# Decode attention and MLP on one core: K tiles two heads ahead of V tiles, one turn moved ahead of the last values, and five matmuls into a spare tile

## The chip, the cores and the metric

The kernel runs on one core of one Trainium2 chip. The metric is the device time of one execution in microseconds (us); lower is better. The profile's span, from the first to the last instruction, is about 1.8 us shorter than that time, because it leaves out what comes before and after. The profiled execution is one of the timed ones, so its own time is known.

Engines in the profile: PE is the matmul engine, PEld its weight loads (they overlap PE), DVE the vector engine, ACT the scalar engine, SP the engine whose queue issues the loads. In the timelines below, the instructions of one engine start in the order of the program.

## The reference, cut to what matters

A decode step, four rows of 576 values: attention over a window of 2048 cached positions, 16 KV heads of 128 with two query heads each, plus an MLP block on the same normalised input.

```python
def _A_ref(x, k_cache, v_cache, wq, wo):                       # attention
    q = (x @ wq).reshape(B, Sq, 32, 128).transpose(0, 2, 1, 3)
    k = jnp.repeat(k_cache[:, :, Sk - W:, :], 2, axis=1)         # W = 2048
    v = jnp.repeat(v_cache[:, :, Sk - W:, :], 2, axis=1)
    p = _softmax(jnp.einsum("bhqd,bhkd->bhqk", q, k) * 128 ** -0.5, axis=-1)
    o = jnp.einsum("bhqk,bhkd->bhqd", p, v)
    return o.transpose(0, 2, 1, 3).reshape(B, Sq, 4096) @ wo
# ... the MLP: x1 = x + shifted part (with one token: zeros); x1 + gelu(layernorm(x1) @ w3) @ w4
return x + _A_ref(xn, ...) + _B_ref(xn, ...)                   # xn = layernorm(x)
```

K and V of the window are 32 tiles of 2 MB (2048 KB each in the profile); with the weights the kernel loads 87.17 MB.

## The kernel before

Loads go through one queue in a fixed order. K and V tiles share six buffers. The order is made here:

```python
order = [("K", 0), ("K", 1), ("K", 2)]
for h in range(Hkv):                       # Hkv = 16
    order.append(("V", h))
    if h + 3 < Hkv:
        order.append(("K", h + 3))         # so: ... K14 V12 K15 V13 V14 V15, then w4
W4_PIECES = [0, 18, 24, 30, 34, 35, 36]    # w4 comes in six loads, the last two of 144 KB
```

A step `t` of the main loop computes scores of head `t`, the softmax of head `t-1` and the product with V of head `t-2`, in four slices. The order of the emissions is the order on each engine:

```python
for t in range(Hkv):
    hm, hv, hf, hp = t - 1, t - 2, t - 3, t - 4
    for s in range(NSL):                   # NSL = 4
        ...
        k_transpose(*divmod(t * NSL + s + 1, NSL))   # DVE: turns the NEXT slice of K ("kt")
        if s == 0:
            if hm >= 0: sm_max(hm)         # DVE: maximum of the scores ("mx", "dm")
            ...
            k_mask(t)
        elif s == 1 and hm >= 0:
            sm_maxT(hm)                    # PE: "mg", needs dm
        ...
        if hv >= 0: pv(hv, s)              # PE: P times V ("O"), needs the V tile
        k_scores(t, s)                     # PE: "S", needs kt
        ...
```

After the last step comes the tail. `hl` is head 15:

```python
    sm_max(hl); sm_rec(hl - 1); o_scale(hl - 2)
    pv(hl - 1, 0); sm_maxT(hl); sm_neg(hl); pv(hl - 1, 1); sm_sub(hl); sm_exp(hl)
    o_turn(hl - 2); pv(hl - 1, 2); pv(hl - 1, 3); o_sum(hl - 2)
    sm_turn(hl); sm_den(hl); sm_rec(hl)    # DVE: PT, which pv(hl) needs
    o_scale(hl - 1)                        # ACT: O_sb of head 14
    for s in range(NSL):
        pv(hl, s)                          # PE: the values of head 15
    o_scale(hl)                            # ACT: O_sb of head 15
    o_turn(hl - 1); o_sum(hl - 1)          # PE: turn ("oT") of head 14; DVE: "on"
    o_turn(hl); o_sum(hl)
    o_spread(hl)                           # PE: "R"
    o_pick(hl)                             # DVE: "mk", "op"
    mlp_out(*pieces[0])                    # PE: 36 matmuls with w4's first piece
    o_proj(hl)                             # PE: 16 matmuls with wo, needs op
    mlp_out(*pieces[1]); mlp_out(*pieces[2]); mlp_out(*pieces[3])
    # ... ACT copies one of two accumulators; pieces 4 and 5 (4 matmuls); DVE adds; store
```

Of the kernel before, what the change touches and what calls it, by code (L numbers as in the profile page):

```python
# [12 lines left out]
F32 = mybir.dt.float32  # L13
# [9 lines left out]
def kernel(  # L23
# [14 lines left out]
    nc = tc.nc  # L38
    P = 128
    B, Sq, D = A_x.shape  # L40
    _, Hkv, Sk, Dh = A_k_cache.shape
# [18 lines left out]
    NW = SC * QD  # L60
# [24 lines left out]
    ps_s = ctx.enter_context(tc.tile_pool(name="ps_s", bufs=2, space=PSUM))  # L85
# [5 lines left out]
    w_tiles = {}  # L91
# [64 lines left out]
    def cleared(shape, name):  # L156
        t = const.tile(shape, BF16, name=name)
        flat = t[:] if len(shape) == 2 else t[:].rearrange("p a b -> p (a b)")
        flat = flat.bitcast(F32)
        nc.scalar.activation(out=flat, in_=zero[:].bitcast(F32).to_broadcast(list(flat.shape)), func=ACT.Copy)  # L160
        return t
# [5 lines left out]
    OR = NI * B  # L167
    OW = OR + NI
    ROWS = slice(NI - 1, NI - 1 + OR, NI)
    gT = cleared([P, NF, OW], "gT")  # L170
# [8 lines left out]
    def acc_matmuls(terms):  # L179
        for i in range(NI):  # L180
            for n, (lhsT, rhs) in enumerate(terms):
                to, q, start = (second[0], QD, second[1]) if second and n % 2 else (acc, 0, False)
                nc.tensor.matmul(out=to[q:q + OR, :], lhsT=lhsT[:, NI - 1 - i:NI - 1 - i + OR],  # L183
                                 rhs=rhs[:, i * CW:(i + 1) * CW], start=start, stop=False, skip_group_check=True)
                if start:
                    second[1] = False
# [119 lines left out]
    for ie in range(4):  # L306
        ib, e = divmod(ie, 2)
        nc.tensor.matmul(out=qs_ps[:, :, ie], lhsT=sel[:, ib, e].rearrange("p k i -> p (k i)"),
                         rhs=q_bf.rearrange("p r g u b -> p (r g u b)"), start=True, stop=True)
# [69 lines left out]
    def sm_rec(h):  # L379
        rd = small.tile([P, 1], F32, tag="rd", bufs=4)  # L380
        nc.vector.reciprocal(out=rd[:], in_=st.pop(("dn", h))[:])
        st["rd", h] = rd

    def pv(h, s):
        if s == 0:
            O_ps[h] = ps_o.tile([P, NSL, Dh], F32, tag="O", name="O")
        vn = kv_tiles["V", h][:].rearrange("p (s c) d -> p s c d", s=NSL)
        for g in range(NQD):
            c = s * NQD + g
            nc.tensor.matmul(out=O_ps[h][g * QD:(g + 1) * QD], lhsT=PT[h][:, c, :], rhs=vn[:, :, c, :],  # L390
                             start=(s == 0), stop=False, skip_group_check=True)
        if s == NSL - 1:
            PT.pop(h)

    def o_scale(h):
        O_sb[h] = bigp.tile([P, NSL, Dh], F32, tag="big", name="O_sb")
        nc.scalar.activation(out=O_sb[h][:], in_=O_ps.pop(h)[:], func=ACT.Copy, scale=st.pop(("rd", h))[:, 0:1])  # L397

    def o_turn(h):
        oT = ps_m.tile([P, NSL, P], F32, tag="m", name="oT")  # L400
        o = O_sb.pop(h)
        for s in range(NSL):
            nc.tensor.transpose(out=oT[:, s, :], in_=o[:, s, :], identity=ident_w[:, s * NJ:s * NJ + P])  # L403
        st["oT", h] = oT

    def o_sum(h):
        oT = st.pop(("oT", h))
        v = oT[:].rearrange("p s (g x) -> p (s g) x", g=NQD)[:, :, 0:NJ].rearrange("p g (b r) -> p b r g", r=rep)
        k = h % WOQ
        if k == 0:  # L410
            st["on"] = small.tile([P, WOH, B], BF16, tag="on", name="on")
        with nc.allow_low_precision("summed in float32"):
            nc.vector.reduce_sum(out=st["on"][:, k * rep:(k + 1) * rep, :].rearrange("p r b -> p b r"),  # L413
                                 in_=v, axis=AX.X)
# [22 lines left out]
    def o_proj(h):  # L437
        if h % WOQ < WOQ - 1:
            return
        for i in range(0, WOR, 2):  # L440
            acc_matmuls([(op[:, i + u, :], wo_tiles[h // WOQ][:, i + u, :]) for u in range(2)])
# [43 lines left out]
    def mlp_out(lo, hi):  # L485
        w4 = w_tiles["w4"]
        for i in range(lo, hi, 2):
            acc_matmuls([(gT[:, u, :], w4[:, u, :]) for u in range(i, min(i + 2, hi))])


    order = [("K", 0), ("K", 1), ("K", 2)]
    for h in range(Hkv):
        order.append(("V", h))
        if h + 3 < Hkv:
            order.append(("K", h + 3))
    W3_AFTER = ("V", 2)
    pos = {"n": 0, "free": NKV}

# [17 lines left out]
# [3 lines that stand above are left out]
            if s == NSL - 1 and hm >= 0:  # L519
                sm_turn(hm)  # L520
            n = t * NSL + s + 1
# [47 lines left out]
    hl = Hkv - 1  # L569
# [14 lines left out]
    sm_den(hl)  # L584
    sm_rec(hl)
    o_scale(hl - 1)
    for s in range(NSL):
        pv(hl, s)
    o_scale(hl)
    o_turn(hl - 1)  # L590
    o_sum(hl - 1)
    pieces = list(zip(W4_PIECES, W4_PIECES[1:]))
    acc_odd = ps_acc.tile([P, CW], F32, tag="g", name="acc_odd")
    second += [acc_odd, True]
# [3 lines left out]
    o_pick(hl)  # L598
    mlp_out(*pieces[0])
    o_proj(hl)  # L600
    mlp_out(*pieces[1])
    mlp_out(*pieces[2])
    mlp_out(*pieces[3])
    second.clear()
    odd = const.tile([OR, CW], F32)
# [39 lines left out]
```

## Time and profile before

| | before |
|---|---|
| time, median of 3 runs at first (6 with the later ones) | 211.63 us (211.54 to 212.5) |
| span of the profiled execution (211.62 us) | 209.8 us |
| PE busy, DVE busy | 71%, 57% |
| loaded, rate over the span | 87.17 MB, 415 GB/s |
| landed: K15, V13 | 179.80, 184.61 us |
| landed: w4's six pieces | 200.48, 202.55, 204.61, 206.00, 206.41, 206.78 us |

The landing times are the last of the sixteen semaphore increments of a load, as the trace records them. The first fence has lines of the profile page of the kernel before: the busy share in 40 equal slices of 5.2 us, in tenths (for PEclk, the granted PE clock in tenths), and the chain of work that ended last, as shares of the span by engine and by line.

```profile
PE   0287496869694009659899599977994926989884
PEclk9999589696969556958999979997999985969999
DMA  7999999999999999999999999999999999999991
DMA 72%; PE 18%; DVE 6%; ACT 1%; issue 1%; SPq 0%; DVEq 0%
DMA vn<-in_A_v_cache_dram 35%; DMA w_sb<-in_B_w_dram 31%; PE S L338 7%; DMA wq_sb<-in_A_wq_dram 6%; DVE kt L225 3%; PE acc L183 2%; PE g_ps L456 2%; PE q_ps L285 2%; PE O L390 2%; PE oT L403 1%; DVE qz L317 1%; PE gT_ps L468 1%; DVE mx L344 1%; PE S L360 1%; ACT q_sb L296 1%
```

The DMA engines are full in every slice but the first and the last, and the chain is mostly waiting for loads. The Trainium skill ("DMA: Bandwidth & Descriptors", "Where 436 GB/s comes from") gives 435 GB/s as the ceiling of the ports into on-chip memory; steady slices of this trace show about 428. So the kernel is bound by its transfers until near the end. What a change of order can touch is the tail.

The next fence is the timeline of PE in the tail of the kernel before. Columns: start, duration, engine, line, operation, output<-inputs, form, count, and in brackets how long PE was idle just before and what ended that.

```profile
184.65 0.57 PE L390 MATMUL O<-vn,PT 128*32 128x512 bf16 x4 [1.55 <-DMA vn<-in_A_v_cache_dram]
185.15 1.89 PE L338 MATMUL S<-kt,qz 128*128 128x512 bf16 x4
186.97 0.18 PE L351 MATMUL mg<-dm,sel_jb 128*8 128x16 bf16 x1
194.41 0.40 PE L390 MATMUL O<-vn,PT 128*32 128x512 bf16 x4
197.92 1.05 PE L390 MATMUL O<-vn,PT 128*32 128x512 bf16 x16
198.90 0.66 PE L403 MATMUL oT<-ident_w,O_sb 128*128 128x128 f32 x4
199.81 0.66 PE L403 MATMUL oT<-ident_w,O_sb 128*128 128x128 f32 x4 [0.26 <-ACT O_sb L397]
200.85 0.35 PE L422 MATMUL R<-on,sel_wo 128*128 128x32 bf16 x8 [0.38 <-DVE on L413]
```

The last step begins when V13 lands at 184.6 (first row) and ends at 194.41, where the tail's first values (head 14) start. The second row: four score matmuls took 1.89 us, while elsewhere they take 1.07. PE was at half clock there. The end of the chain of waits of the same kernel (start, duration, what):

```profile
174.94 31.06 DMA w_sb<-in_B_w_dram
206.00 0.04 issue
206.04 0.28 PE acc L183
...
206.74 0.41 ACT odd L606
```

The last thing that PE waits for is the load of w4's fourth piece. PE was ready for it only about 0.2 us earlier.

### The profile page before, as it was taken

The page shows a single profiled execution, that of the slowest core. Times are in us where ns is not written, and L with a number is a line of the kernel's source. Part 1 is how long each engine was busy: PE and PEld are TensorE (multiplying, and loading weights), DVE is VectorE, ACT ScalarE, POOL GpSimd, SP SyncE. Part 2 cuts the span into 40 slices and gives each one's busy share as a digit, 9 for nine tenths or more (in the row PEclk, how much of TensorE's full clock was granted, in tenths as well). Part 3 has the DMA queues.
Part 4 walks back from the last instruction along what each step waited for, and adds up shares of the span by engine and source line. Part 5 has one row for each costly group of instructions (what it writes and reads, how often), then busy time and mean ns, then how long its engine had stood idle before and what let it go on. Part 6 is the DMA issues. An engine that isn't in the chain of part 4 may idle for free.

```text
span 209.8 us, 2403 instructions
## 1 busy us (share of the span) xinstructions
PE 149.9 (71%) x955; PEld 62.8 (30%) x955; DVE 120.4 (57%) x217; ACT 33.9 (16%) x64; POOL 2.8 (1%) x15
## 2 busy tenths in 40 slices
PE   0287496869694009659899599977994926989884
PEld 0133132223231003214364143332532401425362
DVE  3741899584831082816706869995299471771421
ACT  7602201020211000202102121120111110202300
POOL 4010000000000000000000000000000000000000
PEclk9999589696969556958999979997999985969999
DMA  7999999999999999999999999999999999999991
GB/s 301 400 412 437 428 428 428 436 422 428 469 408 420 433 428 427 438 431 428 431 437 428 422 425 446 425 425 436 422 436 428 421 435 440 425 425 448 418 402 72
DMA packets 6659, 87.32 MB, mean 416 GB/s; under 512 B 748, under 2 KB 1016, under 8 KB 1656
## 3 DMA queue, kind: packets, MB, share of 16 engines
q1 hardware_dynamic: 6640, 87.17, 97.5%
q8 instruction: 7, 0.11, 0.2%
q14 instruction: 4, 0.03, 0.0%
q10 hardware_dynamic: 8, 0.00, 0.0%
HBM read 87.17 MB, written 0.00 MB: 415 GB/s over the span
## 4 chain that ended last, share of the span: by engine, by line
DMA 72%; PE 18%; DVE 6%; ACT 1%; issue 1%; SPq 0%; DVEq 0%
DMA vn<-in_A_v_cache_dram 35%; DMA w_sb<-in_B_w_dram 31%; PE S L338 7%; DMA wq_sb<-in_A_wq_dram 6%; DVE kt L225 3%; PE acc L183 2%; PE g_ps L456 2%; PE q_ps L285 2%; PE O L390 2%; PE oT L403 1%; DVE qz L317 1%; PE gT_ps L468 1%; DVE mx L344 1%; PE S L360 1%; ACT q_sb L296 1%
## 5 line engine op out<-in xcount | busy, mean ns | idle before, releaser
L225 DVE STREAM_TRANSPOSE kt<-kn 128x1024 int32<-128x1024 int32 x64 | 76.4, 1217 | 10.9 <-DMA kn<-in_A_k_cache_dram 10.6
L338 PE MATMUL S<-kt,qz 128*128 128x512 bf16 x256 | 79.7, 441 | 3.1 <-DVE kt L225 3.1
L390 PE MATMUL O<-vn,PT 128*32 128x512 bf16 x256 | 27.4, 426 | 38.9 <-DMA vn<-in_A_v_cache_dram 37.1
L338 PEld LDWEIGHTS <-qz 128*128 128x128 bf16 x256 | 21.7, 104 | 41.5 <-issue 25.8
L366 ACT ACTIVATE E<-S 128x512 bf16<-128x512 f32 x16 | 9.5, 597 | 122.6 <-PE S L360 122.6
L390 PEld LDWEIGHTS <-PT 128*32 128x32 bf16 x256 | 7.2, 94 | 47.3 <-issue 30.2
L372 DVE STREAM_TRANSPOSE PT<-E 128x512 bf16<-128x512 bf16 x16 | 11.4, 710 | 14.9 <-ACT E L366 14.9
L356 DVE TENSOR_REDUCE nm<-mg 8x1 bf16<-8x16 f32 x16 | 2.4, 152 | 20.7 <-PE mg L351 20.7
L397 ACT ACTIVATE O_sb<-O,rd 128x512 f32<-128x512 f32 x16 | 11.0, 686 | 15.6 <-issue 11.0
L413 DVE TENSOR_REDUCE on<-oT 128x8 bf16<-128x128 f32 x16 | 4.5, 280 | 12.7 <-PE oT L403 12.7
L403 PE MATMUL oT<-ident_w,O_sb 128*128 128x128 f32 x64 | 11.1, 302 | 0.3 <-ACT O_sb L397 0.3
L344 DVE TENSOR_REDUCE mx<-S 128x1 f32<-128x512 f32 x16 | 10.5, 657 | 1.3 <-PE S L338 1.3
L403 PEld LDWEIGHTS oT<-ident_w,O_sb 128*128 128x128 f32 x64 | 9.2, 161 | 5.3 <-issue 2.9
L183 PE MATMUL acc<-wo_sb,op 128*8 128x288 bf16 x56 | 7.5, 286 | 0.0
L376 PEld LDWEIGHTS dn<-rs,same_j 128*128 128x128 f32 x32 | 5.8, 188 | 2.9 <-ACT E L366 0.7
L360 PE MATMUL S<-nm,j_row 8*128 8x512 bf16 x16 | 6.5, 409 | 0.0
L329 PE MATMUL S<-negbig,ohT 4*128 4x512 bf16 x16 | 6.2, 385 | 0.0
L351 PE MATMUL mg<-dm,sel_jb 128*8 128x16 bf16 x16 | 2.8, 175 | 3.7 <-DVE dm L346 3.5
L183 PEld LDWEIGHTS <-op 128*8 128x8 bf16 x64 | 4.7, 87 | 2.2 <-issue 0.5
L351 PEld LDWEIGHTS <-sel_jb 128*8 128x8 bf16 x16 | 1.3, 83 | 13.1 <-DVE dm L346 6.5
L183 PE MATMUL acc<-w_sb,gT 128*8 128x288 bf16 x38 | 5.2, 286 | 0.1
L474 DVE COPY g_x<-gT_ps 128x64 f32<-128x64 f32 (+1 forms) x3 | 0.6, 195 | 7.7 <-PE gT_ps L468 7.7
(93 smaller groups left out, 84.3 us busy)
## 6 DMA issues: line engine op xcount, KB each, us to landing
kn<-in_A_k_cache_dram SPq DMA_DIRECT2D x16, 2048.0 KB, 21.9
vn<-in_A_v_cache_dram SPq DMA_DIRECT2D x16, 2048.0 KB, 24.4
wo_sb<-in_A_wo_dram SPq DMA_DIRECT2D x4, 1152.0 KB, 24.5
w_sb<-in_B_w_dram SPq DMA_DIRECT2D x1, 4608.0 KB, 34.3
wq_sb<-in_A_wq_dram SPq DMA_DIRECT2D x1, 4096.0 KB, 12.8
w_sb<-in_B_w_dram SPq DMA_DIRECT2D x1, 2592.0 KB, 31.9
w_sb<-in_B_w_dram SPq DMA_DIRECT2D x2, 864.0 KB, 33.9
w_sb<-in_B_w_dram SPq DMA_DIRECT2D x2, 576.0 KB, 33.0
```

Of the source, the lines that this page charges most:

```text
L183: nc.tensor.matmul(out=to[q:q + OR, :], lhsT=lhsT[:, NI - 1 - i:NI - 1 - i + OR], rhs=rhs[:, i * CW:(i + 1) * CW], start=start, stop=False ...
L225: nc.vector.transpose(out=kt[:], in_=src)
L329: nc.tensor.matmul(out=S_ps[h][:].rearrange("p (c k) -> p c k", k=QD), lhsT=ohT[:], rhs=negbig[:].unsqueeze(1).to_broadcast([B, SC, QD]), ...
L338: nc.tensor.matmul(out=S_ps[h][:], lhsT=qz[:, z0:z0 + P], rhs=kt[:, ib, :, e:2 * QD:2].rearrange("p c k -> p (c k)"), start=False, stop=Fa ...
L344: nc.vector.reduce_max(out=mx[:], in_=S_ps[h][:], axis=AX.X)
L360: nc.tensor.matmul(out=S_ps[h][:], lhsT=j_row[:], rhs=st.pop(("nm", h))[:, 0:1].to_broadcast([NJ, NW]), start=False, stop=False, skip_grou ...
L366: nc.scalar.activation(out=E[h][:].rearrange("p c k -> p (c k)"), in_=S_ps.pop(h)[:], func=ACT.Exp, scale=scale, accum_out=rs[:])
L372: nc.vector.transpose(out=PT[h][:], in_=E.pop(h)[:])
L376: nc.tensor.matmul(out=dn[:], lhsT=same_j[:], rhs=st.pop(("rs", h))[:], start=True, stop=True)
L390: nc.tensor.matmul(out=O_ps[h][g * QD:(g + 1) * QD], lhsT=PT[h][:, c, :], rhs=vn[:, :, c, :], start=(s == 0), stop=False, skip_group_check ...
L397: nc.scalar.activation(out=O_sb[h][:], in_=O_ps.pop(h)[:], func=ACT.Copy, scale=st.pop(("rd", h))[:, 0:1])
L403: nc.tensor.transpose(out=oT[:, s, :], in_=o[:, s, :], identity=ident_w[:, s * NJ:s * NJ + P])
```

## The change

Its intent, read from the edit: let V tiles come a place earlier (K two heads ahead and not three), move a turn out of the way that stood behind the last values, and keep PE's clock up with matmuls into a tile that nobody reads, between pieces of w4. The diff, whole:

```diff
-    order = [("K", 0), ("K", 1), ("K", 2)]
+    order = [("K", 0), ("K", 1)]
     for h in range(Hkv):
         order.append(("V", h))
-        if h + 3 < Hkv:
-            order.append(("K", h + 3))
+        if h + 2 < Hkv:
+            order.append(("K", h + 2))
@@
     o_scale(hl - 1)
+    o_turn(hl - 1)
+    o_sum(hl - 1)
     for s in range(NSL):
         pv(hl, s)
     o_scale(hl)
-    o_turn(hl - 1)
-    o_sum(hl - 1)
@@
     o_proj(hl)
+    warm = ps_s.tile([P, NW], F32, tag="S", name="warm")
+
+    def keep_warm(n):
+        for _ in range(n):
+            nc.tensor.matmul(out=warm[0:OR, :], lhsT=gT[:, 0, 0:OR], rhs=w_tiles["w4"][:, 0, 0:NW],
+                             start=True, stop=True)
+
     mlp_out(*pieces[1])
+    keep_warm(3)
     mlp_out(*pieces[2])
+    keep_warm(2)
     mlp_out(*pieces[3])
```

The last loads become ... V12 K14 V13 K15 V14 V15, then w4: K15 and V13 change places. I call the three parts *order*, *turn* and *spares*.

## The prediction

> **What bounds it now.** The transfers. The page's slices show the DMA engines at 90% or more from the second slice to the last but one; 87.17 MB at 428 GB/s (a steady slice) is 204 us of the 209.8 us span, and the chain of waits is 72% DMA. In the tail the last three pieces of w4 land at 206.00, 206.41 and 206.78 us; the last matmul ends near 207.2, the sum at 207.71, then the store. In the timeline PE has issued all but the last 12 matmuls by 205.8 and waits 0.2 us for the piece that lands at 206.00. PE and the transfers arrive together: the end can hardly get earlier, and PE work added after about 184 us makes it later once 0.2 us are used up.
>
> **The three parts.**
>
> 1. *K two ahead of V.* Same bytes; each step waits for the same place in the stream, where now its K lands, not the V of two heads back. Loads go out a median 22-24 us before landing, so the queue should not run dry. Last step before: V13 lands at 184.61, K15 at 179.80; two of K15's four turns (kt, 1.22 us each) are done by then; PE is busy 9.85 of the 9.90 us from 184.6 to 194.5. After: V13 lands near 179.8, K15 near 184.6. Two kt and head 14's maximum (0.65 + 0.23) then queue on DVE, and head 14's mg, in order on PE, follows near 188.0, before 186.97. The half clock of 184.8-188.2 is partly hidden in that wait. Estimate: step 15 ends 0.7 us later.
>
> 2. *Turn of head 14 ahead of the values of head 15.* Before, pv of head 15 starts at 197.92, right after PT (197.86), and the turn fills a wait for ACT. After, the turn comes first and needs O_sb of head 14, ready at 198.26; its matmuls issue in 0.42 us, so pv starts near 198.7: 0.8 us later, with O_sb, turn, R and w4 behind it.
>
> 3. *Five spare matmuls of 512 columns*, estimated at 0.21 us each (four scores of 512 columns take 1.07 us, 0.21 apart): 1.1 us on PE ahead of the last pieces. The Trainium skill ("TensorE: Matmul & The Clock Gate", "What's actually happening") says that about 3.4 us of busy time bring PE to full clock and an idle window takes it back; this trace agrees (granted 1.0 or 0.5, in pieces of 3.4 us). But it granted 1.0 from 188.2 to the end: nothing to win.
>
> **Sum.** 0.7 + 0.8 + 1.1 - 0.2 of slack = +2.4 us, all on the tail's path; the transfers end when they did. 211.63 becomes about 213.9, +1.1%; range 212.2 to 215.0. Chances: faster by over 2% 0.01, within 2% 0.95, slower by over 2% 0.04.
>
> **What would show it.** Right: w4's last landing still near 206.8; the chain ends in PE, not DMA w_sb, and runs back from a last matmul near 209.5 to DMA kn near 184.6; the first pv of head 15 waits for head 14's O_sb and turn; warm matmuls 0.21 us apart, no wait for w4 after them; DMA rate unchanged. Wrong: the last piece lands over 0.5 us off 206.8; PE waits for w4 after the warm matmuls; pv of head 15 not delayed.
>
> **What would make it wrong.** Another phase of the clock gate (half clock in the last 20 us costs more, full clock at 184-188 less); the queue running dry where K4 now comes behind w3; PE catching up with the transfers; scatter (one of three runs was 212.5).

## The result, and the profile after

The changed kernel took 213.83 us (median of 6 runs, 213.78 to 215.08) against 211.63 us (median of 6, 211.54 to 212.5). The ratio is 1.0107 with a 95% interval of 1.008 to 1.0134. Ratios here and below are the mean time of one kernel's runs over that of the other's of the same rounds, so not quite the ratio of the medians that I quote. Executions over 1.5% slower than the fastest of the same kernel are left out of the means.

The profiled execution of the changed kernel is the slowest of the six, 215.08 us. From the page of the changed kernel, the same lines as above:

```profile
PE   0286595797400888469899599769985958988795
PEclk9999589579955599859999799996999596999699
DMA  7999999999989999999999999999999999999950
DMA 55%; PE 27%; DVE 12%; issue 3%; ACT 2%; SPq 0%; DVEq 0%; ACTq 0%
DMA kn<-in_A_k_cache_dram 49%; PE S L338 9%; DVE kt L225 7%; DMA wq_sb<-in_A_wq_dram 6%; PE acc L183 4%; PE O L390 3%; PE oT L403 3%; PE g_ps L456 2%; DVE mx L344 2%; PE q_ps L285 2%; PE S L360 1%; DVE dm L346 1%; ACT O_sb L397 1%; DVE qz L317 1%; PE gT_ps L468 1%
```

The DMA row is still full, but its last two slices read 5 and 0, where before only the last one fell off: some work is left after the transfers. And w4 is gone from the chain: its pieces landed at 200.33, 202.40, 204.58, 206.00, 206.34 and 206.71 us, as before. The transfers did not become slower; PE ends later. In the chain of waits of the changed kernel the last load is K15 (V13 landed at 179.63, K15 at 184.48):

```profile
159.87 24.61 DMA kn<-in_A_k_cache_dram
184.50 0.04 DVE kt L225
...
210.22 0.41 ACT odd L615
```

From 184.5 on everything is work or waits among the engines. The timeline of PE in the tail of the changed kernel, the rows that answer to those of before, and the spares:

```profile
185.80 1.06 PE L338 MATMUL S<-kt,qz 128*128 128x512 bf16 x4 [0.43 <-DVE kt L225]
187.84 0.17 PE L351 MATMUL mg<-dm,sel_jb 128*8 128x16 bf16 x1 [0.97 <-DVE rd L381]
194.78 0.40 PE L390 MATMUL O<-vn,PT 128*32 128x512 bf16 x4
198.67 1.11 PE L403 MATMUL oT<-ident_w,O_sb 128*128 128x128 f32 x4 [0.53 <-ACT O_sb L397]
199.72 1.90 PE L390 MATMUL O<-vn,PT 128*32 128x512 bf16 x16
203.50 0.35 PE L422 MATMUL R<-on,sel_wo 128*128 128x32 bf16 x8 [0.38 <-DVE on L413]
207.70 0.38 PE L605 MATMUL warm<-w_sb,gT 128*8 128x512 bf16 x1
208.35 0.29 PE L183 MATMUL acc<-w_sb,gT 128*8 128x288 bf16 x1
209.09 0.38 PE L605 MATMUL warm<-w_sb,gT 128*8 128x512 bf16 x1
209.52 0.29 PE L183 MATMUL acc<-w_sb,gT 128*8 128x288 bf16 x1
```

The scores of the last step wait for the first turn of K15, then `mg` waits 0.97 us for head 14's maximum, which DVE does after a second turn (the wait is put down to `rd`, a short instruction just behind it). The turn of head 14 waits for its O_sb, and the values of head 15 come after it. Three spares take from 207.70 to 208.35, two from 209.09 to 209.52: 1.08 us, with no wait for w4 behind them.

Two rows do not fit. The values of head 15 took 1.90 us, and 1.05 before; the turn took 1.11, and 0.66. This execution had a stretch of half clock from 198.5 to 201.9. The two differences make 1.3 us, which is by how much this execution is longer than most of the others. To see the usual execution the changed kernel was run again (e4 below). The fence has one row of the windows view of the changed kernel, then the same window of the second profile. Columns: window, its length, busy us and number of instructions of PE, PEld, DVE, ACT and POOL, the granted clock, the share of DMA, GB/s.

```profile
198.50:201.90 3.40, 2.94 (x20) 1.16 (x20) 0.29 (x1) 0.30 (x2) 0.00 (x0) 0.50 0.95 401
```

```profile
198.50:201.90 3.40, 2.29 (x24) 1.24 (x25) 0.29 (x1) 0.89 (x2) 0.00 (x0) 1.00 0.95 401
```

### The profile page after: what moved, and what is told of

Read it like the earlier page. It is cut to its first block, busy times and chain, and to the rows that moved or that the text cites. A ratio compares the mean times of both kernels' runs of the same rounds, so it can differ in the third digit from the quotient of the medians.

```text
span 213.3 us, 2412 instructions
## 1 busy us (share of the span) xinstructions
PE 152.2 (71%) x960; PEld 64.3 (30%) x960; DVE 120.0 (56%) x217; ACT 33.9 (16%) x64; POOL 2.7 (1%) x15
## 4 chain that ended last, share of the span: by engine, by line
DMA 55%; PE 27%; DVE 12%; issue 3%; ACT 2%; SPq 0%; DVEq 0%; ACTq 0%
DMA kn<-in_A_k_cache_dram 49%; PE S L338 9%; DVE kt L225 7%; DMA wq_sb<-in_A_wq_dram 6%; PE acc L183 4%; PE O L390 3%; PE oT L403 3%; PE g_ps L456 2%; DVE mx L344 2%; PE q_ps L285 2%; PE S L360 1%; DVE dm L346 1%; ACT O_sb L397 1%; DVE qz L317 1%; PE gT_ps L468 1%
## 5 line engine op out<-in xcount | busy, mean ns | idle before, releaser
L338 PEld LDWEIGHTS <-qz 128*128 128x128 bf16 x256 | 22.6, 104 | 73.7 <-issue 58.1
L403 PE MATMUL oT<-ident_w,O_sb 128*128 128x128 f32 x64 | 12.0, 320 | 1.4 <-ACT O_sb L397 1.4
L390 PEld LDWEIGHTS <-PT 128*32 128x32 bf16 x256 | 6.7, 96 | 11.1 <-issue 10.3
L183 PE MATMUL acc_odd<-w_sb,gT 128*8 128x288 bf16 x34 | 5.1, 286 | 0.0
L456 PE MATMUL g_ps<-w_sb,ln2T 128*32 128x512 bf16 (+1 forms) x50 | 4.9, 445 | 0.0
```

Source lines behind the costliest of these rows:

```text
L183: nc.tensor.matmul(out=to[q:q + OR, :], lhsT=lhsT[:, NI - 1 - i:NI - 1 - i + OR], rhs=rhs[:, i * CW:(i + 1) * CW], start=start, stop=False ...
L338: nc.tensor.matmul(out=S_ps[h][:], lhsT=qz[:, z0:z0 + P], rhs=kt[:, ib, :, e:2 * QD:2].rearrange("p c k -> p (c k)"), start=False, stop=Fa ...
L390: nc.tensor.matmul(out=O_ps[h][g * QD:(g + 1) * QD], lhsT=PT[h][:, c, :], rhs=vn[:, :, c, :], start=(s == 0), stop=False, skip_group_check ...
L403: nc.tensor.transpose(out=oT[:, s, :], in_=o[:, s, :], identity=ident_w[:, s * NJ:s * NJ + P])
L456: nc.tensor.matmul(out=g_ps[g * QD:(g + 1) * QD], lhsT=ln2T[:, k, :], rhs=rhs, start=(j == 0), stop=False, skip_group_check=True)
```

## The experiments

The sum of the prediction came out, +2.2 us against +2.4. That does not show that its terms are right. The theory at this point: three delays add up on PE's path, and the transfers end when they did. Rival A: the new order hurts the transfers or starves their queue. Rival B: the clock gate falls differently and that is the whole loss. Each kernel was run in five rounds with the kernel before on the same chip; the kernel before had 211.46 to 212.51, 211.44 to 212.46 and 211.48 to 212.51 us in the three groups of runs, with medians of 211.69, 211.66 and 211.67. All twelve passed the comparison with the reference; for the three that leave out work, that only shows that the left-out terms are smaller than its tolerance.

### One part alone

**e1, order only.**

```diff
-    order = [("K", 0), ("K", 1), ("K", 2)]
+    order = [("K", 0), ("K", 1)]
     # ... and h + 2 for h + 3, as in the change; nothing else
```

> Only the load order of the change (K two heads ahead). Theory (the tail of PE is delayed and the transfers are not): the profiled changed kernel ended its last step 0.37 us later than before (194.78 against 194.41), and PE had 0.24 us of slack before w4's fourth piece landed, so +0.1 us (0.0 to 0.4): 211.7 to 212.0. Rival A (the new order itself slows the transfers or starves their queue): most of the +2.2 us shows here, 213 or more, and w4 lands later than 206.8. Rival B (all of it is a clock gate that falls differently): a half-clock piece in the last 20 us here, and +1 us or more.

Measured: 211.84 us (211.71 to 211.99), ratio 1.0004 (0.9986 to 1.0023). Rival A falls for the order by itself: w4's last piece landed at 206.69.

**e2, turn only.**

```diff
     o_scale(hl - 1)
+    o_turn(hl - 1)
+    o_sum(hl - 1)
     for s in range(NSL):
         pv(hl, s)
     o_scale(hl)
-    o_turn(hl - 1)
-    o_sum(hl - 1)
```

> Only head 14's turn moved ahead of head 15's values. Theory: the first values of head 15 start 0.8 us later (they wait for the scaled output of head 14 and then for its four turn matmuls), less 0.24 us of slack: +0.55 us, 212.2 (212.0 to 212.5), with full clock in the tail. If the longer idle time of PE before the turn makes the clock fall to half, +1.3 us more in some executions. Rivals A and B: no change beyond 0.1 us without a half-clock piece.

Measured: 211.80 us (211.45 to 213.21), ratio 1.0010 (0.9986 to 1.0035). The expected +0.55 us did not come.

**e3, spares only.**

```diff
     mlp_out(*pieces[1])
+    keep_warm(3)
     mlp_out(*pieces[2])
+    keep_warm(2)
     mlp_out(*pieces[3])
```

> Only the five spare matmuls. Theory: 5 x 0.216 us = 1.08 us of PE work in its one queue, less 0.24 us of slack: +0.85 us, 212.5 (212.2 to 212.7); w4's last landing still near 206.8. The idea behind the change (they keep the clock up or fill waits for the transfers for nothing): 211.6 or less.

Measured: 211.91 us (211.65 to 213.38), ratio 1.0017 (0.9991 to 1.0043). The expected +0.85 us did not come either.

**e4, the changed kernel again.** No edit.

> The changed kernel once more, for its profile: the profiled execution of it (215.08) had a half-clock piece from 198.5 to 201.9 us that its other runs (213.8) seem not to have had. Theory: +2.2 us, 213.8, and in an execution at full clock in the tail the values of head 15 take 1.05 us and not 1.90, head 14's turn 0.66 and not 1.11; those two differences are the 1.25 us by which the profiled one is longer. Rival B: every execution has the half-clock piece in the tail.

Measured: 214.12 us (213.68 to 216.38), ratio 1.0132 (1.0096 to 1.0169). Its profile is of an execution of 213.84 us at full clock from 180.5 to the end. Two rows of its timeline:

```profile
198.75 0.66 PE L403 MATMUL oT<-ident_w,O_sb 128*128 128x128 f32 x4 [0.53 <-ACT O_sb L397]
199.34 1.05 PE L390 MATMUL O<-vn,PT 128*32 128x512 bf16 x16
```

The 0.66 and 1.05 us are back, so the half clock explains the slow profile, and rival B falls: +2.2 us remain without it.

So each part alone costs almost nothing and all three cost 2.2 us. The theory's delays are there in the traces (the rows above), so what must be wrong is the slack: there has to be far more of it than the 0.2 us that I read. The profile of e3 shows where. It runs the same code as the kernel before up to w4, and its profiled execution took 211.66 us. PE in its timeline:

```profile
184.56 0.40 PE L390 MATMUL O<-vn,PT 128*32 128x512 bf16 x4 [1.36 <-DMA vn<-in_A_v_cache_dram]
184.89 1.08 PE L338 MATMUL S<-kt,qz 128*128 128x512 bf16 x4
185.89 0.17 PE L351 MATMUL mg<-dm,sel_jb 128*8 128x16 bf16 x1
192.84 0.40 PE L390 MATMUL O<-vn,PT 128*32 128x512 bf16 x4
199.28 0.35 PE L422 MATMUL R<-on,sel_wo 128*128 128x32 bf16 x8 [0.38 <-DVE on L413]
200.37 0.28 PE L183 MATMUL acc<-w_sb,gT 128*8 128x288 bf16 x1 [0.74 <-DMA w_sb<-in_B_w_dram]
```

Here the last step starts at the same 184.6 but ends at 192.84 and not at 194.41. Windows of the kernel before and of e3 over the start of that step, one fence each, tell why:

```profile
184.60:188.20 3.60, 3.55 (x15) 0.91 (x15) 2.81 (x5) 0.00 (x0) 0.00 (x0) 0.53 1.02 437
```

```profile
184.60:188.20 3.60, 3.60 (x26) 1.65 (x26) 3.36 (x6) 0.00 (x0) 0.00 (x0) 1.00 1.01 432
```

The one profile that I had of the kernel before ran this step at half clock (0.53 against 1.00, 15 matmuls and not 26 in 3.6 us). At full clock the step takes 1.5 us less (192.84 - 184.51 = 8.3 us from V13's landing, against 194.41 - 184.61 = 9.8), and PE then waits in two places. In front, 0.74 us for w4's first piece (last row above). Behind, for the third and the fourth piece: in e3 the spares start at 204.29, where the second piece's matmuls are done; w4's third piece had landed at 204.52 and the fourth at 205.95. Without spares PE would have waited until 204.56, worked 0.73 us and waited again until 205.99: 0.27 + 0.70 = 0.97 us behind. This last number is worked out from the row times of e3. The profile of e2, also at full clock there, lets it be checked. Its turn uses up the wait in front and 0.23 us of this one, so 0.74 us should be left. PE could start the fourth piece's matmuls at 205.47, and starts when the piece has landed (206.09):

```profile
206.13 0.28 PE L183 MATMUL acc<-w_sb,gT 128*8 128x288 bf16 x1 [0.49 <-DMA w_sb<-in_B_w_dram]
```

That is 0.66 us (the bracket counts from the modelled end of the matmul before), and with 0.06 us for the third piece 0.72.

With the same profiles the costs at full clock can be measured anew. Order: the last step, from the landing that starts it to its end, takes 194.78 - 184.48 = 10.3 us after and 192.84 - 184.51 = 8.3 us in e3, so 2.0 us. The first scores start 0.91 us later (185.80 and 184.89); with the wait of `mg` it is 1.95 us (187.84 and 185.89). Turn: from the end of the last step to R it is 202.27 - 194.86 = 7.41 us in e4 and 199.28 - 192.84 = 6.44 in e3, so 0.97 us. Spares: 1.08 us.

### Parts together, and PE's work taken away

**e5, order and turn.** The change without its third part.

```diff
-    warm = ps_s.tile([P, NW], F32, tag="S", name="warm")
-    # ... keep_warm
     mlp_out(*pieces[1])
-    keep_warm(3)
     mlp_out(*pieces[2])
-    keep_warm(2)
     mlp_out(*pieces[3])
```

> The change without its five spare matmuls. Theory (costs add on PE, and the slack of 0.24 us is used once): 0.37 + 0.8 - 0.24 = +0.9 us, 212.5 (212.2 to 213.0); so the spare matmuls are worth the other 1.1 to 1.2 us of the change's +2.2 us. If they fill a wait, this is as slow as the whole change, 213.8.

Measured: 212.64, 212.79, 214.07, 214.16, 214.20 us, and one run of 216.97 that counts as slow and is left out; ratio 1.0086 (1.0058 to 1.0115). The expected 212.5 is near the two fastest only. The profiled execution (214.20) has half clock from 198.8 to 202.3, and its values of head 15 took 1.90 us; so the upper group fits the half clock, though only one of its runs was profiled.

**e6, ten spares on the kernel before.**

```diff
     mlp_out(*pieces[1])
+    keep_warm(6)
     mlp_out(*pieces[2])
+    keep_warm(4)
```

> The kernel before with ten spare matmuls (six and four). Theory: 10 x 0.216 - 0.24 = +1.9 us, 213.5 (213.2 to 213.8): the slope from five to ten is 1.08 us, and a straight line through five and ten meets zero at about one spare matmul. If they raise the clock, less than twice the five.

Measured: 213.07 us (212.82 to 213.47), ratio 1.0062 (1.0046 to 1.0079). Five spares cost 0.2 us by the medians and ten cost 1.4: there is a kink, and it lies at about five. With 0.97 us of waits behind, five (1.08) just fill them and ten (2.16) leave 1.2. The expectation had put the kink at one spare.

**e7, the kernel before with less work on PE** (wrong).

```diff
-    mlp_out(*pieces[0])
```

> The kernel before without the 36 matmuls of w4's first piece (the piece is still loaded; the result is wrong on purpose): PE has 2.2 us less to do in the tail. Theory (the transfers end at 206.8 whatever PE does, and only 0.3 us of arithmetic hangs on the last piece): 211.4 to 211.7, no gain over 0.2 us. Rival (PE bounds the tail): 209.5 to 210.

Measured: 211.66 us (211.49 to 212.77), ratio 1.0001 (0.9983 to 1.0019). Taking 36 matmuls away, 2.2 us of PE, gains nothing: the kernel before stands on its transfers. Of 6 runs 2 were slower, 212.42 and 212.77. The second was profiled, and it had half clock from 205.3 to 208.7, over the last matmuls, after a stretch in which PE was mostly waiting for w4. In the piece of 3.41 us ahead of it PE was busy for 1.46 us. That is the case for which spares are made; the one profile of the whole kernel before does not show it.

**e8, the changed kernel with less work on PE** (wrong): the same line removed.

> The changed kernel without the same 36 matmuls (wrong on purpose). Theory: PE is 2.0 us late at the fourth piece in the changed kernel, and this gives 2.2 us back: it catches up with the transfers, 211.5 to 211.9, the time of the kernel before. Rival A (the new order slows the transfers): still over 212.5.

Measured: 212.64, 212.75, 214.37, 214.44 us, and 215.86 and 215.92 that count as slow; ratio of the fast ones 1.0085 (1.0051 to 1.0119). This missed, and by a flaw of the experiment. Without those 36 matmuls the wo matmuls wait 0.97 us for `op` from DVE, which the 36 had hidden, so not 2.2 but about 1.2 us is given back (2.2 - 0.97; from R to the first wo matmul it is 1.32 us in this profile, and 2.49 in the changed kernel's). The two fastest runs are 1.0 us below the changed kernel's fastest, 213.68. Less work on PE also brings more half clock: the profile has it twice, from 198.8 and again from 205.6.

**e12, mended.** The last wo matmuls are left out too (wrong).

```diff
-    mlp_out(*pieces[0])
-    o_proj(hl)
```

> Mends the run without w4's first matmuls, which gave back only 1.0 us, since the last wo matmuls then waited for DVE (0.97 us) that those matmuls had hidden. Here the last wo matmuls are left out as well (wrong on purpose): 36 and 16 matmuls, 3.06 us less on PE's path. Theory: PE catches up with the transfers, 211.5 to 211.9 (half clock in the tail: up to 213). Rival (the new order slows the transfers): still 212.5 or more in all executions, with the last landing of w4 later than 207.

Measured: 211.89 us (211.53 to 212.22), ratio 1.0002 (0.9986 to 1.0017). With 3.2 us less on PE (52 matmuls that take from 203.78 to 206.97 in the profile of the changed kernel; the expectation's 3.06 was low) the changed kernel is back at the time of the kernel before, and w4's last piece landed at 206.67. Rival A falls for the whole change.

**e10, order and spares**, without the turn: the order's edit and the third part's.

> Order and spares without the turn. Theory: 2.0 + 1.1 - 1.8 = +1.3 us, 212.9 at full clock (212.6 to 213.2), 1.3 us more where half clock falls into the tail; so the turn is worth the missing 0.8 us. If the turn is free (as it was alone), 213.8.

Measured: 213.35 us (212.72 to 214.26), ratio 1.0076 (1.0051 to 1.0100). The fastest runs are where the theory put them, about 1.0 us below those of the whole change: the turn is worth that here, and nothing alone. The spread upward is only partly explained. Its profile is of a run of 213.70 us with full clock in the tail, and it shows another reason: the loads landed late. K15 landed at 185.40, 0.92 us later than in the changed kernel (184.48), and the scores start at 186.72, 0.92 us later than 185.80:

```profile
185.42 2.37 DVE L225 STREAM_TRANSPOSE kt<-kn 128x1024 int32<-128x1024 int32 x2 [1.05 <-DMA kn<-in_A_k_cache_dram]
```

The first of K15's sixteen increments came at 182.83, as in the changed kernel (182.73), and the last 2.57 us after it, not 1.75. w4's last piece landed at 207.58; in the other thirteen profiles it landed between 206.61 and 206.96. That is one execution; whether the new order has a part in it is not shown. PE was later still, so the run ended with PE.

**e9, the last pair of loads put back** in the changed kernel.

```diff
         if h + 2 < Hkv:
             order.append(("K", h + 2))
+    at = order.index(("V", Hkv - 3))
+    order[at:at + 2] = [("K", Hkv - 1), ("V", Hkv - 3)]
```

> The changed kernel whole, but with the last K (head 15) loaded ahead of V of head 13 again, as before; all earlier loads stay as changed. Theory after eight runs: at full clock the new order costs 1.9 to 2.0 us, all in the last step, because head 15's K now lands last and PE waits twice, for its first turn (0.95 us) and for head 14's maximum behind the second turn (0.97 us); the kernel before has about 1.8 us of slack at full clock. So the order's cost goes and the turn (0.8) and the spares (1.1) fit into the slack: +0.1 us, 211.5 to 212.2 (up to 213 in executions with half clock in the tail). Rival (the order costs something all along the stream, or in the transfers): stays near 213.8.

Measured: 212.49 us (211.87 to 212.82), ratio 1.0032 (1.0013 to 1.0051). Against the whole change (medians 213.83 and 214.12) this gives back 1.3 to 1.6 us; between the fastest runs (213.68 and 211.87) it is 1.8. So the order's cost sits in one pair of loads, the last K and the V before it; in the 28 K and V tiles loaded before the pair the new order costs nothing that shows in the fastest runs. The median is above the range that I expected for full clock; two runs (211.87 and 211.89) are in it. The profile is of one at full clock, and the rest were not profiled.

**e11, the five spares moved into the last softmax**, on order and turn. They use `qz`, which is loaded by then, and not w4.

```diff
     pv(hl - 1, 0)
+    keep_warm(3)
     sm_maxT(hl)
     # ...
     sm_den(hl)
+    keep_warm(2)
     sm_rec(hl)
     o_scale(hl - 1)
```

> Order and turn, with the five spare matmuls moved to where PE waits in the last softmax: three ahead of head 15's mg, where PE is idle 0.72 us, and two ahead of head 14's turn, idle 0.53 us. Theory of the clock: a stretch of some 3.4 us with much idle time in the last softmax is followed, where the free-running stretches fall so, by 3.4 us at half clock, which costs 1.3 us in order-and-turn (four of six executions 214 or more, two near 212.7). If the spares fill that, nearly all executions are 212.6 to 212.9. Rival (spares do nothing for the clock): a mix of 212.7 and 214.1 as without them.

Measured: 212.75, 212.77, 212.85, 213.02, 213.43, 214.14 us; ratio 1.0063 (1.0042 to 1.0085). From the timeline of PE:

```profile
195.17 0.81 PE L574 MATMUL warm<-qz 128*8 128x512 bf16 x3
196.06 0.17 PE L351 MATMUL mg<-dm,sel_jb 128*8 128x16 bf16 x1
198.23 0.59 PE L574 MATMUL warm<-qz 128*8 128x512 bf16 x2
198.83 0.66 PE L403 MATMUL oT<-ident_w,O_sb 128*128 128x128 f32 x4
```

Here the same five matmuls cost nothing: in e4 `mg` ran at 195.98 and the turn at 198.75. This shows that place and not number made the spares costly. As for the clock, its pieces lie on a grid of 3.41 us whose place differs from run to run (half clock began at 198.52 in the changed kernel's profile, at 196.41 in e6's), so only counting runs can tell. One execution of six was at 214 or more, and four of six in e5, which has no spares. That points the way the theory says, but with six runs each it is not shown.

### The terms against the runs

One table with the terms at full clock (order 2.0, turn 0.97, spares 1.08 per five; waits that absorb them: 0.74 in front of w4 and 0.97 behind; spares come too late for the front one). The measured column is the fastest run of each kernel over 211.5, the fastest of the kernel before (211.44 to 211.54 in its groups). The fastest run is taken because the two disturbances that the profiles show, half clock and a late landing, lengthen a run. The terms come from the profiles of the changed kernel, e3 and e4, so the other rows test them.

| kernel | worked out | measured |
|---|---|---|
| order (e1) | 2.0 - 1.71 = 0.3 | 0.2 |
| turn (e2) | 0.97 < 1.71: 0 | 0.0 |
| spares (e3) | 1.08 - 0.97 = 0.1 | 0.15 |
| ten spares (e6) | 2.16 - 0.97 = 1.2 | 1.3 |
| order, turn (e5) | 2.97 - 1.71 = 1.3 | 1.1 |
| order, spares (e10) | 3.08 - 1.71 = 1.4 | 1.2 |
| turn, spares (e9) | 0.97 - 0.74 + 1.08 - 0.97 = 0.3 | 0.4 |
| all three (e4) | 4.05 - 1.71 = 2.3 | 2.2 |

All agree within 0.2 us. No version beat the kernel before, and none of the parts could: e7 shows that PE's tail is not what holds it.

## Why the prediction was right or wrong

Right: the time (213.9, measured 213.83), the direction, and that the transfers would not move (last landing 206.71, predicted 206.8). Right in mechanism: PE waits for the turn of K15 and for head 14's maximum behind a second turn (`mg` near 188.0, measured 187.84); head 15's values wait for head 14's O_sb and turn; the spares stand 0.21 us apart with no wait for w4 after them; the chain runs back to K15 near 184.6.

Two terms of its sum were mis-sized, and the errors nearly cancel. Both come from one stretch of half clock, worth 1.5 us, in the only profile of the kernel before: it made the order look about that much cheaper and the slack about that much smaller. So the sum was safe for the three parts together, where PE ends last, and not for a single part. The prediction did not say so; that it came out is to that extent luck.

- *"Estimate: step 15 ends 0.7 us later."* At full clock it is 2.0 us. Against the profile of before it is even less than predicted, 0.37 us (194.78 and 194.41), but that profile had half clock there, worth 1.5 us.
- *"once 0.2 us are used up", "- 0.2 of slack".* At full clock there are about 1.7 us: 0.74 in front of w4's first piece (seen) and 0.97 behind it (worked out). This is the step that failed. I read slack off one profiled execution that happened to have used up most of it, and took it for a property of the kernel. Had I been asked for any one part alone from this sum, I would have been wrong: e2 and e3 were expected at +0.55 and +0.85 and came at +0.1 and +0.2.
- *Turn, 0.8 us:* 0.97 at full clock. *Spares, 1.1 us:* 1.08.
- *"nothing to win"* from the clock: for spares at that place it holds, since they stand behind the half clock that fell at 198.5 in the profiled execution. But "granted 1.0 from 188.2 to the end" was again one execution's phase: of the fourteen profiles, five have a half-clock stretch between 195 and 209 us.

The sum therefore should have read 2.0 + 0.97 + 1.08 - 1.7 = 2.3. There is one more loss, which the sum leaves out and the list of what would make it wrong names: half clock late in the run. The kernel before hid a stretch of it, worth 1.5 us, in its waits (the profiled execution took 211.62 us). The changed kernel has none of these waits left, and its profiled execution shows 1.3 us in full (215.08). Its other slow runs (215.36, 216.38) were not profiled, so their cause is not shown.

## What to carry to other kernels

In a kernel bound by its transfers, price a delay against the waits that stand between it and the end, and count those waits in an execution whose clock you have checked; several small delays that are free one at a time can cost their full sum together. The order in which operands land should end with the one that needs the least work before its first use: here V feeds PE at once, while K first needs a turn on another engine. If matmuls are added to keep PE busy, put them where PE waits anyway; the same five cost about 1 us behind the wait and nothing inside it.

## What the Trainium skill lacked or had wrong

- "TensorE: Matmul & The Clock Gate", section "What's actually happening": it says that the clock falls after an idle window of about 3.4 us. A later section of it tells of a kernel in which short gaps made the clock swing, without a measure. Pieces of that length are what the traces show, but they need not be idle. The first fence is of the changed kernel just ahead of its half clock, the second of e6, the third of e4, which kept full clock in the piece after it, though PE was busy for less of it.

```profile
195.10:198.50 3.40, 2.30 (x24) 1.03 (x20) 1.97 (x7) 1.25 (x3) 0.00 (x0) 1.00 1.03 441
```

```profile
193.00:196.40 3.40, 2.51 (x28) 1.11 (x28) 2.11 (x7) 1.12 (x3) 0.00 (x0) 1.00 1.02 438
196.40:199.80 3.40, 3.40 (x24) 1.88 (x25) 0.29 (x1) 0.95 (x2) 0.00 (x0) 0.50 0.94 399
```

```profile
163.50:166.90 3.40, 1.98 (x12) 0.81 (x13) 3.37 (x8) 0.00 (x0) 0.00 (x0) 1.00 1.04 445
166.90:170.30 3.40, 3.40 (x24) 1.66 (x23) 2.10 (x5) 1.18 (x3) 0.00 (x0) 1.00 1.00 429
```

  PE was busy 2.30 of 3.40 us and 2.51 of 3.40 us and the clock fell; it was busy 1.98 of 3.40 and the clock stayed. So busy time as the profile counts it does not give the rule; what does is left open.
- Same page, same section: it calls the phase of these pieces run-variable, and the runs agree (the grid above). It puts the cost of the ramp at the start under 1% of a typical kernel; a stretch of half clock in the tail, which it does not price, cost 1.3 us of 213.8 here, 0.6%. What it lacks is that this decides how much slack a single profile seems to show (0.2 or 1.7 us here), which is as much as any part of the change.
- "DMA: Bandwidth & Descriptors", section "Where 436 GB/s comes from": it says that for loads the memory side binds, at about 358 GB/s. Taken alone, that sentence is wrong for this kernel: its trace has steady slices of 428 GB/s and 415 GB/s over the whole span, all read from device memory, so the ceiling of 435 fits better (single slices scatter, from 400 to 469). The lines just above that section, with a measured load of 425 and 358 only where both cores of a pair stream, agree with this run on one core.
- The same page, section "Why a DMA increments its semaphore by 16 and not by 1", says that the engines of one load finish independently, and the trace agrees; it gives no spread. In the kernel before, the sixteen increments of K0 came within 0.45 us (18.42 to 18.87), those of w4's last piece within 1.85 us (204.93 to 206.78), eight by 205.5 and eight after 206.3. The whole kernel waits for the last. In one execution (e10) the spread of the last loads was 2.6 us. The profile counts seven packets on a queue for instructions, of 16 KB and about 0.9 us each; that they drive the engines apart is only a guess, and no run tested it.
